# Moving VectorE's sums, one score group and the first tile's units in a pooled-attention plus feed-forward kernel

## Chip, cores, metric

The kernel runs on one core of one Trainium2 chip. The metric is the device time of one execution in microseconds (us). Executions of one kernel differ (the six of the kernel before in the comparison lie between 292.65 and 294.22 us), so medians of several are given. A profile shows one execution; its span is about 1.8 us shorter than the device time of the same execution (292.4 against 294.17).

## What is computed

Inputs q, k, v have the shape (8 batches, 8 heads, 576 positions, 64). Cut to what matters:

```python
k_p = k.reshape(B, H, 72, 8, D).mean(axis=3)       # pool 8 positions
v_p = v.reshape(B, H, 72, 8, D).mean(axis=3)
attn = softmax(scale * q @ k_p.T)                  # 576 x 72 per head
x = (attn @ v_p) as 4608 tokens x 512
h = x @ w_in                                       # 512 -> 2048
out = (h * cos(h)) @ w_out                         # 2048 -> 512
```

## The kernel before

The tokens go through in nine tiles of 512 (t=0 to 8). A tile has an **up stage** (128x512 matmuls by w_in, cosine on ScalarE, multiply on VectorE, which gives g) and a **down stage** (g by w_out). From t=1 on the down stage uses seven half-size products in place of eight, which need sums of quarters of g (g1 to g4) and of w_out; VectorE makes the sums of g, each in two halves (0 and 1). Between the products of tile t TensorE does the attention of batch t+1 in units u0 to u3 (scores, exponential on ScalarE, values, a multiply on VectorE that writes xT and frees a bank of PSUM, the memory that TensorE writes to) and a rest unit of batch t. GpSimd meanwhile pools k and v of batch t+2.

```python
def put_g12(i):                                     # two sums of 128x1024 bf16 each call
    f0, f1 = 4 * i, 4 * i + 4
    vec = nc.vector.tensor_tensor
    vec(out=g1[:, f0:f1], in0=g_part(0, 1, f0, f1), in1=g_part(1, 1, f0, f1), op=ADD)
    vec(out=g2[:, f0:f1], in0=g1[:, f0:f1], in1=g_part(0, 0, f0, f1), op=SUB)
# put_g3(i): g3 = g_part(0,0) - g_part(0,1);  put_g4(i): g4 = g_part(1,0) - g2
# ... in the up stage, after step n of 8 ...
if t == 1 and n == 6:
    put_g12(0)
if t > 1 and 3 <= n < 6:
    (put_g12, put_g3, put_g4)[n - 3](0)
# ... the down stage of t >= 1 (cut) ...
u0, u1, u2, u3 = [(b, us[i], banks[j]) for i, j in enumerate((2, 1, 0, 1))]
ur = (t, REST, banks[2])
product(0)
scores_of(u0, u1, u2)            # u2 needs bank 0, which the last multiply of g frees
product(1)
put_g12(1)
reads[0]()                       # copy of the first product out of PSUM (p_sb)
for i in range(0 if t == 1 else 1, 2):
    put_g3(i)
reads[1]()
for i in range(0 if t == 1 else 1, 2):
    put_g4(i)
values(*u0, later)
product(2); reads[2](); muls()   # muls: the multiply of the unit before
values(*u1, later)
product(3); reads[3](); muls()
values(*u2, later)
product(4); reads[4](); muls()
scores_of(ur, u3)                # u3 needs bank 1, which the multiply of u1 frees
# ... product(5) with the values of ur and u3 inside, product(6) ...
# ... the down stage of t == 0: (matmul number, unit) in order ...
fill = [(1, REST scores), (2, S0), (8, pool v), (8, REST values), (11, S1), (13, V0), (18, S2), ...]
```

The softmax here doesn't subtract the row's maximum and nothing guards it: scores larger than these inputs give would overflow.

## Time and profile before

| | before |
|---|---|
| device time, median (first 3 runs; with the 3 of the comparison) | 293.3 us; 293.49 us |
| TensorE busy in the profile | 280.6 of 292.4 us |
| VectorE, ScalarE, GpSimd busy | 79%, 71%, 51% |
| first tile's down stage | 20.24 us |
| down stage of t=1 | 18.42 us |
| a steady tile, start to start | 29.93 us |

A timeline line has start and duration in us, engine, line of the kernel, output and inputs, shape, count, and in brackets the idle time of the engine before it with what ended that. I take a tile's start as that of its first up matmul in TensorE's timeline; all stage lengths are differences of such starts.

The wait of 0.89 us at t=1 has its cause on VectorE. This is VectorE's timeline of the kernel before, at the end of the up stage of t=1:

```profile
66.74 1.23 DVE L331 TENSOR_TENSOR g_sb<-bank,cos 128x1024 bf16<-128x1024 f32 x1 [0.50 <-ACT cos L327]
67.88 0.68 DVE L359 TENSOR_TENSOR g<-g_sb 128x1024 bf16<-128x1024 bf16 x1
68.59 0.69 DVE L360 TENSOR_TENSOR g<-g,g_sb 128x1024 bf16<-128x1024 bf16 x1
69.20 1.22 DVE L331 TENSOR_TENSOR g_sb<-bank,cos 128x1024 bf16<-128x1024 f32 x1
```

Two sums (L359, L360) run before the last multiply, which frees the bank of the third score group.

### The profile page before, as it was taken

How to read it: one execution, taken by the hardware profiler on the slowest of the kernel's cores; microseconds unless marked ns; L12 is line 12 of the kernel's file. 1: busy time of each engine (PE TensorE's matmuls, PEld its weight loads, DVE VectorE, ACT ScalarE, POOL GpSimd, SP SyncE). 2: the span in 40 equal slices, each digit the busy share in tenths (PEclk: the TensorE clock that was granted, in tenths of full speed). 3: DMA queues.
4: the chain of work that ended last, by engine and by line, in shares of the span. 5: the costliest groups of instructions: out<-in, count | busy, mean ns of one | idle time of the engine just before them, and what ended most of it. 6: DMA issues, size and time to landing. Idle time of an engine off the chain costs nothing. (4 is left out here: it accounts for less than half of the span.)

```text
span 292.4 us, 5446 instructions
## 1 busy us (share of the span) xinstructions
PE 280.6 (96%) x2168; PEld 178.1 (61%) x2168; DVE 232.4 (79%) x314; ACT 208.1 (71%) x265; POOL 149.9 (51%) x145
## 2 busy tenths in 40 slices
PE   6989999998899999999999999999999999999994
PEld 2545544446764587458745884488547854884583
DVE  6458638879987988799879986988798879955972
ACT  3886888368877799679976987699769876536600
POOL 8553089993996359836983699329920000000000
PEclk9999999999999999999999999999999999999998
DMA  7999999557819692969196916694680050006014
GB/s 156 198 207 206 206 205 210 116 92 110 136 35 201 60 167 42 204 88 166 26 194 94 177 27 137 116 164 77 138 112 0 4 126 18 2 2 144 0 38 108
DMA packets 44489, 32.97 MB, mean 113 GB/s; under 512 B 22192, under 2 KB 40112, under 8 KB 44464
## 3 DMA queue, kind: packets, MB, share of 16 engines
q0 software_dynamic: 19744, 18.07, 39.4%
q1 hardware_dynamic: 24080, 14.03, 23.5%
q10 hardware_dynamic: 640, 0.52, 0.7%
q8 instruction: 17, 0.28, 0.4%
q14 instruction: 8, 0.07, 0.1%
HBM read 36.70 MB, written 9.44 MB: 158 GB/s over the span
## 5 line engine op out<-in xcount | busy, mean ns | idle before, releaser
L317 PE MATMUL bank<-xT,w_in_sb 128*128 128x512 bf16 x512 | 113.8, 379 | 0.0
L327 ACT ACTIVATE cos<-bank,half_pi 128x1024 f32<-128x1024 f32 x64 | 70.3, 1113 | 46.9 <-PE bank L317 46.3
L317 PEld LDWEIGHTS <-w_in_sb 128*128 128x128 bf16 x576 | 56.1, 98 | 65.8 <-issue 0.4
L331 DVE TENSOR_TENSOR g_sb<-bank,cos 128x1024 bf16<-128x1024 f32 x64 | 77.3, 1220 | 22.5 <-ACT cos L327 22.4
L151 POOL TENSOR_TENSOR half_sums<-kv_st 72x512 f32<-72x512 bf16 x48 | 57.6, 1228 | 26.1 <-DMA kv_st<-in_k_dram 25.7
L262 DVE TENSOR_TENSOR xT<-bank,inv 64x512 bf16<-64x512 f32 (+1 forms) x72 | 45.3, 629 | 12.9 <-ACT inv L258 11.8
L398 PEld LDWEIGHTS <-g 128*128 128x128 bf16 x512 | 49.0, 98 | 6.9 <-issue 1.2
L257 ACT ACTIVATE inv<-bank 64x512 f32<-64x512 f32 (+1 forms) x72 | 39.1, 544 | 11.9 <-PE bank L251 11.0
L398 PE MATMUL obank<-w,g 128*128 128x256 bf16 x368 | 43.6, 273 | 0.0
L398 PEld LDWEIGHTS <-g_sb 128*128 128x128 bf16 x384 | 36.8, 98 | 7.3 <-issue 1.2
L229 ACT ACTIVATE ex<-bank 72x1024 bf16<-72x1024 f32 (+1 forms) x40 | 35.2, 929 | 3.5 <-PE bank L222 3.3
L153 POOL TENSOR_TENSOR half_sums<-half_sums 72x512 f32<-72x512 f32 x24 | 29.9, 1267 | 0.0
L398 PE MATMUL obank<-w_out_sb,g_sb 128*128 128x256 bf16 x240 | 28.7, 273 | 0.0
L258 ACT ACTIVATE inv<-inv 128x512 f32<-128x512 f32 (+1 forms) x36 | 21.0, 583 | 1.1
L251 PE MATMUL bank<-ex,vz 72*128 72x256 bf16 (+1 forms) x176 | 20.1, 243 | 0.0
L222 PE MATMUL bank<-qT,kk 64*72 64x256 bf16 (+1 forms) x192 | 13.7, 252 | 3.4 <-DVE xT L262 1.7
L334 PE MATMUL obank<-w_out_sb,g_sb 128*128 128x512 bf16 x64 | 15.7, 380 | 0.7 <-DMA w_out_sb<-in_moe_w_out_dram 0.7
L251 PEld LDWEIGHTS <-vz 72*128 72x128 bf16 x176 | 13.7, 97 | 3.2 <-DVE xT L262 0.5
L156 POOL TENSOR_TENSOR kp<-half_sums 72x512 bf16<-72x512 f32 x12 | 15.4, 1304 | 0.5
L398 PE MATMUL obank<-w_out_sb,g 128*128 128x256 bf16 x112 | 15.6, 273 | 0.0
L398 PE MATMUL obank<-w,g_sb 128*128 128x256 bf16 x128 | 15.3, 273 | 0.0
L317 PE MATMUL obank<-xT,w_in_sb 128*128 128x512 bf16 x64 | 15.1, 379 | 0.0
(86 smaller groups left out, 254.9 us busy)
## 6 DMA issues: line engine op xcount, KB each, us to landing
out_dram<-o_two SPq DMA_DIRECT2D x64, 128.0 KB, 2.4
kv_st<-in_v_dram POOLq DMA_DIRECT2D x8, 576.0 KB, 13.0
kv_st<-in_k_dram POOLq DMA_DIRECT2D x7, 576.0 KB, 7.6
q_b<-in_q_dram POOLq DMA_DIRECT2D x6, 576.0 KB, 10.0
w_in_sb<-in_moe_w_in_dram POOLq DMA_DIRECT2D x4, 512.0 KB, 14.0
w_out_sb<-in_moe_w_out_dram POOLq DMA_DIRECT2D x4, 512.0 KB, 18.4
q_b<-in_q_dram POOLq DMA_DIRECT2D x4, 288.0 KB, 12.4
g_sb<-in_k_dram SPq DMA_DIRECT2D x1, 576.0 KB, 3.4
```

The lines of the kernel that those rows point to most:

```text
L151: add(out=s[:, h:h + 2], in0=x[:, h:h + 2, 0:4, :], in1=x[:, h:h + 2, 4:8, :], op=ADD)
L153: add(out=s[:, h:h + 4, 0:2, :], in0=s[:, h:h + 4, 0:2, :], in1=s[:, h:h + 4, 2:4, :], op=ADD)
L229: nc.scalar.activation(out=ex[:, 0:nh * n].rearrange("p (a n) -> p a n", a=2), in_=pair[:Sp, :, 0:nh * n // 2], func=ACTF.Exp, scale=scale ...
L251: nc.tensor.matmul(pair[:, hp, (i // 2) * n:(i // 2 + 1) * n], lhsT=vz[b % 2][:, pj, 2 * hp:2 * hp + 2, :].rearrange("p a d -> p (a d)"), ...
L257: nc.scalar.activation(out=inv[half[1 - hp]], in_=pair[half[1 - hp], hp, 0:w], func=ACTF.Ln)
L258: nc.scalar.activation(out=inv, in_=inv, func=ACTF.Exp, scale=-1.0)
L262: nc.vector.tensor_mul(out=x_out(b, u, half[hp]), in0=cols(pair[half[hp], hp, :], u), in1=cols(inv[half[1 - hp]], u))
L317: nc.tensor.matmul(h[j] if h is obanks else h[:, j, :], lhsT=w_in_sb[fc // 4][:, ki, (fc % 4) * 128:(fc % 4 + 1) * 128], rhs=xT[:, ki, t * ...
L327: nc.scalar.activation(out=c, in_=ps, func=ACTF.Sin, bias=half_pi[:, :1])
L331: nc.vector.tensor_mul(out=o, in0=ps, in1=c)
L334: nc.tensor.matmul(o, lhsT=g_sb[:, fc, ms * 128:(ms + 1) * 128], rhs=w_out_sb[fc // 4][:, fc % 4, :], start=(fc == 0), stop=(fc == FFCH - 1))
L398: mms.append(lambda bank=bank, first=first, g=g, w=w, fc=fc, p=p: nc.tensor.matmul(bank[p], lhsT=g(fc, p), rhs=w(fc), start=(first and fc ...
```

## The change

Its intent is to take the waits of TensorE away. It has four parts, called A to D here. **A**: `product(1, 0, 2)` before the scores, so these come two matmuls later. **B**: other places for the sums of half 0 at t=1. **C**: g4 of half 1 behind the multiplies of u1, in every tile. **D**: in the first tile, REST scores and S0 in one group, and S1 and V0 ahead of the ninth w_out matmul.

```diff
--- before.py
+++ after.py
@@ -353,19 +353,16 @@
     def g_part(f, t, f0, f1):
         return g_sb[:, f * HF + f0:f * HF + f1, t * HT:(t + 1) * HT]
 
-    def put_g12(i):
+    def put_g(k, i):
         f0, f1 = 4 * i, 4 * i + 4
-        vec = nc.vector.tensor_tensor
-        vec(out=g1[:, f0:f1], in0=g_part(0, 1, f0, f1), in1=g_part(1, 1, f0, f1), op=ADD)
-        vec(out=g2[:, f0:f1], in0=g1[:, f0:f1], in1=g_part(0, 0, f0, f1), op=SUB)
-
-    def put_g3(i):
-        f0, f1 = 4 * i, 4 * i + 4
-        nc.vector.tensor_tensor(out=g3[:, f0:f1], in0=g_part(0, 0, f0, f1), in1=g_part(0, 1, f0, f1), op=SUB)
-
-    def put_g4(i):
-        f0, f1 = 4 * i, 4 * i + 4
-        nc.vector.tensor_tensor(out=g4[:, f0:f1], in0=g_part(1, 0, f0, f1), in1=g2[:, f0:f1], op=SUB)
+        t1f1, t1f2, t2f1, t2f2 = [g_part(f, t, f0, f1) for t in range(2) for f in range(2)]
+        out, x, y, op = {1: (g1, t2f1, t2f2, ADD), 2: (g2, g1[:, f0:f1], t1f1, SUB), 3: (g3, t1f1, t2f1, SUB),
+                         4: (g4, t1f2, g2[:, f0:f1], SUB)}[k]
+        nc.vector.tensor_tensor(out=out[:, f0:f1], in0=x, in1=y, op=op)
+
+    def put_gs(*kis):
+        for k, i in kis:
+            put_g(k, i)
 
     def down_products(t):
 
@@ -543,10 +540,8 @@
                     puts[0](vec)
                     between = ((puts[1], act),)
             up_g(t, fp, between)
-            if t == 1 and n == 6:
-                put_g12(0)
-            if t > 1 and 3 <= n < 6:
-                (put_g12, put_g3, put_g4)[n - 3](0)
+            if 0 < t and 3 <= n < 6:
+                put_gs(*[(k, 0) for k in (((3,), (1,), ()) if t == 1 else ((1, 2), (3,), (4,)))[n - 3]])
             if 0 < t and b < B:
                 if n == 0:
                     q_transpose(b)
@@ -571,9 +566,10 @@
             exp_tables()
             fill = [(1, lambda: scores(t, REST, banks[2])), (16, lambda: values(t, REST, banks[1]))]
         if t == 0:
-            fill[1:] = [(2, S_(0, 0)), (8, lambda: pool_v_mm(1, banks[1])), (8, lambda: values(t, REST, banks[2])),
-                        (11, S_(1, 0)), (13, V_(0, 1)), (18, S_(2, 2)), (21, V_(1, 0, later)), (26, S_(3, 1)),
-                        (32, lambda: later.pop()()), (32, V_(2, 2)), (40, V_(3, 0))]
+            fill = [(2, fill[0][1]), (2, S_(0, 0)), (8, lambda: pool_v_mm(1, banks[1])),
+                    (8, lambda: values(t, REST, banks[2])), (8, S_(1, 0)), (8, V_(0, 1)),
+                    (18, S_(2, 2)), (21, V_(1, 0, later)), (26, S_(3, 1)), (32, lambda: later.pop()()),
+                    (32, V_(2, 2)), (40, V_(3, 0))]
         if t < FIRST:
             fi = 0
             for n, (ms, fc) in enumerate(mms):
@@ -615,18 +611,20 @@
             if rest:
                 exp_tables()
             product(0)
+            product(1, 0, 2)
             if steady:
                 scores_of(u0, u1, u2)
             elif rest:
                 scores_of(ur)
-            product(1)
-            put_g12(1)
+            product(1, 2)
+            if t == 1:
+                put_g(2, 0)
+            put_gs((1, 1), (2, 1))
             reads[0]()
-            for i in range(0 if t == 1 else 1, 2):
-                put_g3(i)
+            put_g(3, 1)
             reads[1]()
-            for i in range(0 if t == 1 else 1, 2):
-                put_g4(i)
+            if t == 1:
+                put_g(4, 0)
             if steady:
                 values(*u0, later)
             product(2)
@@ -637,6 +635,7 @@
             product(3)
             reads[3]()
             muls()
+            put_g(4, 1)
             if steady:
                 values(*u2, later)
             product(4)
```

I also built A, B, C and D as four edits of the kernel before. Their edits, shown with the experiments e1 (A), e2 (B), e3 (C) and e4 (D), together give the changed kernel's order of instructions, so the four parts are the whole change.

## The prediction

> **What bounds the kernel now.** I read the engine table first, then the list of TensorE's waits, then TensorE's timeline tile by tile. The table has each engine's busy time and share of the span.
>
> ```profile
> span 292.4 us, 5446 instructions
> PE 280.6 (96%) x2168; PEld 178.1 (61%) x2168; DVE 232.4 (79%) x314; ACT 208.1 (71%) x265; POOL 149.9 (51%) x145
> ```
>
> TensorE is the bound, and it is not busy for 292.4 - 280.6 = 11.8 us. The tail after its last matmul takes 292.4 - 288.4 = 4.0 us and the start 1.5 us; the change touches neither. The list of waits (total, times, longest) says what the rest is:
>
> ```profile
> PE bank L222 <- DVE xT L262: 1.7, 2, 1.4
> PE bank L222 <- DVE g_sb L331: 1.7, 6, 0.9
> PE obank L494 <- DVE g L438: 1.5, 1, 1.5
> PE obank L334 <- DMA w_out_sb<-in_moe_w_out_dram: 0.7, 1, 0.7
> ```
>
> The score matmuls (L222) of the next batch wait until VectorE has emptied the PSUM bank that they write. The timeline (start, duration, instructions, idle before) places these waits: first the second tile (t=1), then a steady one (t=2).
>
> ```profile
> 67.12 1.91 PE L398 MATMUL obank<-w_out_sb,g_sb 128*128 128x256 bf16 x16
> 68.96 0.63 PE L222 MATMUL bank<-qT,kk 64*72 64x256 bf16 x8
> 70.47 0.41 PE L222 MATMUL bank<-qT,kk 64*72 64x256 bf16 x4 [0.89 <-DVE g_sb L331]
> ...
> 81.01 0.41 PE L222 MATMUL bank<-qT,kk 64*72 64x256 bf16 x4 [1.40 <-DVE xT L262]
> ...
> 99.35 1.91 PE L398 MATMUL obank<-w_out_sb,g_sb 128*128 128x256 bf16 x16
> 101.19 0.63 PE L222 MATMUL bank<-qT,kk 64*72 64x256 bf16 x8
> 101.98 0.41 PE L222 MATMUL bank<-qT,kk 64*72 64x256 bf16 x4 [0.16 <-DVE g_sb L331]
> ```
>
> The 0.16 comes again in each of t=2 to 6, and at t=4 there is one more wait of 0.29 for an xT multiply. At t=7 and t=8 the trace shows no wait. So the change can reach at most 0.89 + 1.40 + 5 x 0.16 + 0.29 + 0.70 = **4.1 us**, 1.4% of 293.3.
>
> **What the Trainium skill says.** "Perfetto Trace Analysis", Optimization Strategy: look for the gaps on the bounding engine and for what releases them. That is the method here. "TensorEngine Tiling (Array Packing)", Key Properties: a change of tiling mode drains TensorE. The trace agrees: the 16 matmuls at 67.12 hand over to 64-row scores after 1.84 us, while the 16 at 70.81 hand over to 72-row ones after 1.76, so a switch costs about 0.09. "SBUF — State Buffer", Who interferes with whom: a VectorE instruction with two SBUF inputs contends with GpSimd instructions that read SBUF. The trace agrees: a sum over g of 128x1024 bf16 takes 0.68 us, but the two at 74.19 took 2.60 together, beside GpSimd's additions from 73.33.
>
> **The change part by part.**
>
> *A. First score group two matmuls later (t=1 to 6).* Two matmuls of 128x256 at 1.75/16 = 0.109 us, so 0.22 us, move ahead of the scores. In a steady tile the scores then start at 101.41 instead of 101.19, and the third group is due 0.63 later, at 102.04. Its bank is free at 100.70 + 1.22 = 101.92, and the group started 0.06 after that before. No wait is left. The number of mode switches stays. Gain 5 x 0.16 = **0.8 us** for t=2 to 6.
>
> *B. Other order on VectorE at t=1.* Before, the sums g1 and g2 of the first half ran at 67.88 to 69.28, ahead of the last multiply of g (69.20), whose cosine was ready at 68.44. They delayed it by 0.7. In the new order g3 and g1 of that half go into gaps in which VectorE waits for cosines (0.93 us idle before 63.28, 0.50 before 65.01), and g2 goes behind the multiply. That now runs from 68.49 to about 69.72. The third group is due at 68.96 + 0.22 + 0.63 = 69.8. Its wait of 0.89 goes.
>
> The second wait, 1.40, is for the multiply of the second unit, which ended at 79.57 + 1.39 = 80.96. I walk VectorE with starts 0.61 apart for independent sums and 0.73 for dependent ones: last multiply 68.49, g2 69.63, g1 70.24, g2 70.97, copy of the first product 71.58 to 72.27, g3, a read, g4 of the first half (0.7 alone, up to 1.3 beside GpSimd), a read to 75.4 at the latest, two multiplies to 76.8, a read to 77.5 (its product ends at 76.3), two multiplies to 78.95. TensorE wants that bank at about 78.8. So 1.40 shrinks to between 0 and 0.2. A **new wait** appears: the third product overwrites the bank that the copy reads until 72.27, and TensorE would be there at 72.11, so 0.2. Net at t=1: 0.89 + 1.40 - 0.2 - 0.15 = **1.95**, and with 0.1 of rounding either way I take 2.0 us.
>
> *C. g4 of the second half later (t=1 to 8).* One sum of 0.68 us leaves the place before the third read and goes behind the multiplies of the second unit. At t=4 this ends the 0.29 wait: two sums there took 1.67 and 1.04 instead of 0.68. Gain **0.3**. The price: at t=2 the sum now starts at about 110.6, beside GpSimd's additions (110.09 to 112.6), and its first reader, the ninth matmul of the sixth product (the built program waits there, not at the first), comes at about 112.1. With 0.68 it ends at 111.3; contended, with 1.3 to 1.8, at 111.9 to 112.4. I charge 0.05 to 0.1 for each of four tiles, **-0.3**. At t=6 and t=8 GpSimd is idle.
>
> *D. First tile.* The merged scores save one mode switch, 0.1, but then the pooling matmuls meet a bank that VectorE frees at 34.41 + 1.23 = 35.64 (they started at 35.69 before), so nothing comes of it. The two units moved forward fill the 0.70 wait for w_out group 2:
>
> ```profile
> 37.91 0.81 PE L334 MATMUL obank<-w_out_sb,g_sb 128*128 128x512 bf16 x3 [0.70 <-DMA w_out_sb<-in_moe_w_out_dram]
> 38.65 0.41 PE L222 MATMUL bank<-qT,kk 64*72 64x256 bf16 x4
> ```
>
> The scores run at 37.25 to 37.6, the values wait for pooled v (36.97 + 0.69 = 37.66) and end at 38.15, and w_out matmuls go on from there. Eight of them (8 x 0.216 = 1.73) reach group 1 at 39.9, where the kernel before was at 40.5. But group 1 has hardly landed: the transfers are back to back on a saturated queue (206 GB/s around there); one group is 0.524 MB, so 2.5 us, and I estimate from the landing of group 2 at 37.9 that groups 1 and 3 land at 40.45 and 43.0. Before, TensorE reached group 3 at 43.13 without a recorded wait. So the wait moves from group 2 to groups 1 and 3, and the gain is **0.1** of a possible 0.6.
>
> Sum: 0.8 + 2.0 + 0.3 - 0.3 + 0.1 = 2.9 us, so 293.3 - 2.9 = **290.4 us**.
>
> **The rivals.**
>
> 1. *All gaps close:* both transfers are early enough (0.4 more), no contention (0.3 more), t=1 perfect (0.3 more): 289.4. For it: each wait has one releaser, and VectorE is only 79% busy. Against: D's queue runs at its rate whatever TensorE does.
>
> 2. *VectorE gives it back:* g4 blocks behind GpSimd in every steady tile, the sixth product waits 0.3, and the later multiplies push the unit of the next tile (xT was ready at 117.14, its reader came at about 117.2, so slack is 0.06). That would lose 0.5 in each of four tiles: 292.4. For it: two weight sums at 54.1 and 55.9 beside GpSimd took 1.78 and 1.64. Against: after g4 ScalarE's chain sets the last multiplies anyway (idle 0.92 and 0.30 before them), which leaves VectorE 1.2 us of play.
>
> 3. *TensorE is not truly idle in the gaps:* its ends are modelled, so a wait of 0.16 may be partly an artefact. For it: "busy" is modelled. Against: the starts of the groups are recorded, and tiles with and without the extra 0.29 differ by it (29.93 against 30.33 us over two neighbouring tile starts, with t=4 also slower in its loads). This would make it 291.
>
> **Range and chances.** The runs before spread from 292.65 to 294.22, so a median of few may be 0.5 off. With rivals 1 and 2 at the ends plus some noise: 289.2 to 291.9. Faster by over 2% needs 5.9 us, more than all reachable waits together (4.1): 2%. Slower by over 2% would need a stall of a kind that the trace doesn't show: 1%.
>
> **What would show each step.** A: no wait of scores on g_sb at t=2 to 6, and tiles of about 13.81 + 15.96 = 29.77 us instead of 29.93. B: t=1's second half (67.12 to 85.54 before) takes 16.2 to 16.6 instead of 18.42 us, with a new wait of about 0.2 on the p_sb copy. C: the g4 instruction takes over 0.68 us at t=2 to 5 and TensorE waits for it little or not at all. D: the wait for w_out still totals 0.4 to 0.7, now at groups 1 and 3, and TensorE reaches t=1 at 53.2 rather than at 53.30. If w_out's wait vanishes, D is wrong upwards; if the sixth product waits for g4, or the first product of a tile for xT, C is wrong downwards.

## The result

The changed kernel takes **291.08 us** in the median (290.17 to 291.33, 6 runs), the kernel before 293.49 (292.65 to 294.22, 6 runs). The ratio is 0.9914, 95% interval 0.9893 to 0.9935. A ratio here is the mean time of one kernel's runs over that of the other's of the same rounds, so not quite the ratio of the medians. Executions over 1.5% slower than the fastest of the same kernel are left out of the means.

The engine table of the changed kernel, and its list of TensorE's waits (total, times, longest), with the start left out:

```profile
span 289.3 us, 5446 instructions
PE 281.1 (97%) x2168; PEld 178.5 (62%) x2168; DVE 233.1 (81%) x314; ACT 208.0 (72%) x265; POOL 149.9 (52%) x145
...
PE obank L395 <- DVE g_sb L331: 0.3, 1, 0.3
...
PE obank L334 <- DMA w_out_sb<-in_moe_w_out_dram: 0.2, 1, 0.2
```

The waits of score groups on g_sb and xT are gone. A new one on g_sb has come, and the one for w_out is smaller. TensorE's timeline of the changed kernel, t=1 first and t=2 after it:

```profile
67.36 2.13 PE L395 MATMUL obank<-w_out_sb,g_sb 128*128 128x256 bf16 x18
69.42 0.98 PE L222 MATMUL bank<-qT,kk 64*72 64x256 bf16 x12
...
71.87 0.60 PE L251 MATMUL bank<-ex,vz 72*128 72x256 bf16 x4
72.52 1.91 PE L395 MATMUL obank<-w,g 128*128 128x256 bf16 x16
...
78.72 0.55 PE L222 MATMUL bank<-qT,kk 64*72 64x64 bf16 x12
...
97.38 1.47 PE L395 MATMUL obank<-w_out_sb,g_sb 128*128 128x256 bf16 x12
99.13 0.83 PE L395 MATMUL obank<-w_out_sb,g_sb 128*128 128x256 bf16 x6 [0.27 <-DVE g_sb L331]
```

All twelve score matmuls of u0 to u2 now run in one piece (69.42), as do those of ur and u3 (78.72). Before the third product there is a gap that is too short for the list: the values at 71.87 take 4 x 0.109 = 0.44 us, so it could start at 72.31 and starts at 72.52. At t=2 the first product itself now waits 0.27.

Lengths of stages in us from TensorE's timelines, for the two kernels and for all experiments (t1 start is counted from the span's start):

| run | t0 down | t1 start | t1 down | t2 up | t2 down | t3 whole | t4 whole | span |
|---|---|---|---|---|---|---|---|---|
| before | 20.24 | 53.30 | 18.42 | 13.81 | 16.12 | 29.93 | 30.33 | 292.4 |
| changed, first | 19.96 | 53.55 | 16.11 | 13.91 | 16.21 | 29.72 | 29.71 | 289.3 |
| changed, after_again | 19.62 | 53.05 | 16.10 | 14.33 | 16.26 | 30.09 | 29.71 | 289.6 |
| changed, after_third | 19.61 | 52.77 | 16.10 | 14.24 | 16.21 | 29.99 | 29.71 | 289.1 |
| e1 (A alone) | 19.38 | 52.91 | 18.06 | 13.82 | 15.90 | 29.71 | 29.71 | 290.1 |
| e2 (B alone) | 19.38 | 53.45 | 16.25 | 13.94 | 16.36 | 29.94 | 29.93 | 290.3 |
| e3 (C alone) | 19.37 | 53.63 | 17.03 | 14.19 | 16.12 | 29.93 | 29.93 | 291.3 |
| e4 (D alone) | 20.13 | 52.93 | 18.48 | 13.82 | 16.12 | 29.93 | 29.93 | 291.7 |
| no_vz_add_t1 | 20.13 | 53.64 | 16.11 | 13.81 | 15.98 | 30.08 | 29.72 | 289.6 |
| after_no_w_out_wait | 19.61 | 52.81 | 16.10 | 14.07 | 16.39 | 30.08 | 29.72 | 289.2 |
| v1_both | 19.61 | 52.90 | 16.08 | 14.38 | 15.90 | 30.03 | 29.72 | 289.1 |
| f1 (changed without C) | 20.15 | 53.61 | 16.25 | 13.81 | 15.90 | 29.71 | 29.71 | 289.1 |
| f2 (C only from t=4) | 19.61 | 53.11 | 16.25 | 13.81 | 16.14 | 29.72 | 29.71 | 288.8 |
| f3 (f2 without D) | 19.62 | 52.81 | 16.25 | 14.12 | 16.25 | 29.71 | 29.71 | 288.9 |

In the first two profiles the span fell by 3.1 us. By stages: the start to the first w_out matmul lost 0.53 (33.06 to 33.59, code that the change does not touch), t0's down stage gained 0.28, t1's 2.31; t=2 lost 0.10 in its up and 0.09 in its down stage; t=3, 5 and 6 gained 0.21 to 0.22 each and t=4 0.62. The median time fell by only 2.41, because the profiled execution of before (294.17) was slower than the median of its kind.

### The profile page after: what moved, and what is told of

Read it like the earlier page. It is cut to its first block, busy times and chain, and to the rows that moved or that the text cites. A ratio compares the mean times of both kernels' runs of the same rounds, so it can differ in the third digit from the quotient of the medians.

```text
span 289.3 us, 5446 instructions
## 1 busy us (share of the span) xinstructions
PE 281.1 (97%) x2168; PEld 178.5 (62%) x2168; DVE 233.1 (81%) x314; ACT 208.0 (72%) x265; POOL 149.9 (52%) x145
## 4 chain that ended last, share of the span: by engine, by line
PE 70%; DVE 3%; ACT 0%; issue 0%
PE obank L395 31%; PE bank L317 27%; PE bank L251 4%; PE obank L317 4%; PE bank L222 3%; DVE g_sb L331 2%; PE bank L395 2%; DVE g L361 1%; ACT cos L327 0%; DVE o_two L411 0%
## 5 line engine op out<-in xcount | busy, mean ns | idle before, releaser
L151 POOL TENSOR_TENSOR half_sums<-kv_st 72x512 f32<-72x512 bf16 x48 | 54.5, 1162 | 26.2 <-DMA kv_st<-in_k_dram 25.8
L153 POOL TENSOR_TENSOR half_sums<-half_sums 72x512 f32<-72x512 f32 x24 | 31.8, 1345 | 0.0
L361 DVE TENSOR_TENSOR g<-g_sb 128x1024 bf16<-128x1024 bf16 x32 | 23.7, 740 | 0.5
L156 POOL TENSOR_TENSOR kp<-half_sums 72x512 bf16<-72x512 f32 x12 | 16.4, 1389 | 0.5
```

What stands on the lines that cost most here:

```text
L151: add(out=s[:, h:h + 2], in0=x[:, h:h + 2, 0:4, :], in1=x[:, h:h + 2, 4:8, :], op=ADD)
L153: add(out=s[:, h:h + 4, 0:2, :], in0=s[:, h:h + 4, 0:2, :], in1=s[:, h:h + 4, 2:4, :], op=ADD)
L361: nc.vector.tensor_tensor(out=out[:, f0:f1], in0=x, in1=y, op=op)
```

## The experiments

The theory at this point: A and B work as written, C's and D's gains are small, and the 0.27 at t=2 is a collision of VectorE with GpSimd. The rivals: the gain of t=1 is C's and not B's; C is a loss; D is worth its 0.6 us; the 0.27 is VectorE's own work.

### The four parts one at a time

All four ran on one chip against 11 runs of the kernel before (median 293.58, 292.77 to 294.64).

**A alone.**

```diff
             product(0)
+            product(1, 0, 2)
             if steady:
                 scores_of(u0, u1, u2)
             elif rest:
                 scores_of(ur)
-            product(1)
+            product(1, 2)
```

> Only the first score group moved two matmuls later. Theory: the 0.16 us wait of the third score group goes at t=2 to 6, so these tiles take 29.72 us from start to start instead of 29.93 (5 x 0.2 = 1.0 us), while t=1 gains nothing: its two waits end when VectorE is done (0.89 becomes about 0.67 because TensorE arrives 0.22 later, and the 1.40 stays as long as VectorE's chain sets it). Sum about 1.0 us of 293.5. Rival: the shift only moves idle time, because VectorE is late by a fixed amount after it: then t=2 to 6 stay at 29.93.

Measured: 292.52 us (292.03 to 293.34), ratio 0.9963 (0.9941 to 0.9985), so 0.0037 x 293.6 = 1.1 us. The waits of e1 at t=1, in TensorE's timeline:

```profile
70.08 0.41 PE L222 MATMUL bank<-qT,kk 64*72 64x256 bf16 x4 [0.67 <-DVE g_sb L331]
80.26 0.41 PE L222 MATMUL bank<-qT,kk 64*72 64x256 bf16 x4 [1.32 <-DVE xT L262]
```

The first wait shrank by exactly the two matmuls, 0.22, as expected. At t=2 to 6 no score group waits and the down stages take 15.90 instead of 16.12 us. So A is worth 5 x 0.22 = 1.1 us; the 0.16 that the waits showed was not the whole gap. I had expected nothing at t=1 and its stage got 0.36 shorter. VectorE's timeline of e1 shows where:

```profile
73.80 2.23 DVE L368 TENSOR_TENSOR g<-g_sb,g 128x1024 bf16<-128x1024 bf16 x2
```

In the kernel before this pair of sums took 2.60 us (74.19), so all that follows, the multiply that ends the second wait too, came 0.37 earlier. GpSimd's additions, which wait for their load, began at 73.83 in e1 and at 73.33 before, so the collision was a shorter one. Whether A brings that or the load's time is chance is not shown.

**B alone.** The third change, in the down stage, puts g2 of half 0 between `product(1)` and the sums of half 1, at t=1 only.

```diff
-            if t == 1 and n == 6:
-                put_g12(0)
+            if t == 1 and n == 3:
+                put_g3(0)
+            if t == 1 and n == 4:
+                g1 of half 0
 ...
-            for i in range(0 if t == 1 else 1, 2):
-                put_g3(i)
+            put_g3(1)
```

> Only the new places of g1, g2, g3 of the first half at t=1; g4 of both halves stays together before the third read. Theory: the wait of 0.89 shrinks to 0.1 to 0.2 (the last multiply ends 0.7 earlier), the wait of 1.40 shrinks to 0.3 to 0.7 because only the sums and not the last g4 have left the chain. t=1's second half takes 16.8 to 17.4 instead of 18.42 us, tiles 2 to 6 stay at 29.93. Sum about 1.2 us. Rival: the whole gain of t=1 comes from g4 of the second half; then this run gains 0.9 at most.

Measured: 292.16 us (290.98 to 292.68), ratio 0.9942 (0.9918 to 0.9965), 1.7 us. The waits of e2 in TensorE's timeline of t=1 and t=2:

```profile
69.89 0.41 PE L222 MATMUL bank<-qT,kk 64*72 64x256 bf16 x4 [0.16 <-DVE g_sb L331]
99.20 0.61 PE L398 MATMUL obank<-w_out_sb,g_sb 128*128 128x256 bf16 x4 [0.28 <-DVE g_sb L331]
```

t=1 gained 2.17 in its down stage, more than I expected: the wait of 1.40 is wholly gone without C. The rival that t=1 is C's gain falls. And the 0.28 at t=2 appears here, without C and without A: it comes with B.

**C alone.**

```diff
-            for i in range(0 if t == 1 else 1, 2):
-                put_g4(i)
+            if t == 1:
+                put_g4(0)
 ...
             reads[3]()
             muls()
+            put_g4(1)
```

> Only g4 of the second half moved behind the multiplies of the second unit, at t=1 to 8. Theory: at t=1 the 0.89 stays, the 1.40 shrinks by the sum's 0.7 to 1.3 us, to 0.1 to 0.7; at t=4 the wait of 0.29 (if this execution has it) is gone; TensorE never waits for the late g4 although it takes over 0.68 us beside GpSimd's additions at t=2 to 5. Sum 0.7 to 1.3 us. Rival (as predicted): each collision with GpSimd costs TensorE 0.05 to 0.1, so t=2 to 5 get longer than 29.93.

Measured: 292.78 us (292.24 to 293.08), ratio 0.9967 (0.9946 to 0.9987), 1.0 us. C alone takes the 1.40 away too (t=1's down stage 17.03). It gives 0.38 back in the up stage of t=2. Here are TensorE, then VectorE, GpSimd and ScalarE of e3 around that place:

```profile
80.79 1.22 PE L398 MATMUL obank<-w_out_sb,g 128*128 128x256 bf16 x8
...
86.57 3.61 PE L317 MATMUL bank<-xT,w_in_sb 128*128 128x512 bf16 x16 [0.21 <-DVE xT L262]
```

```profile
79.62 1.72 DVE L368 TENSOR_TENSOR g<-g_sb,g 128x1024 bf16<-128x1024 bf16 x1
...
85.13 1.39 DVE L262 TENSOR_TENSOR xT<-bank,inv 64x512 bf16<-64x512 f32 x2
```

```profile
79.53 2.94 POOL L153 TENSOR_TENSOR half_sums<-half_sums 72x512 f32<-72x512 f32 x2
```

```profile
83.91 0.63 ACT L258 ACTIVATE inv<-inv 128x512 f32<-128x512 f32 x1
```

The late g4 starts 0.09 us after a pair of GpSimd's additions and takes 1.72 instead of 0.68. All that VectorE does after it is late: the multiplies of u3 had their input at 83.91 + 0.63 = 84.54 and start at 85.13. The first up matmuls of t=2 that read this part of xT wait for them. The sixth product, where I had put the cost, came late too: the eight matmuls that hold its ninth one took 1.22 us instead of the usual 1.04, a wait of 0.18 at t=1 that the list does not show. So TensorE did wait for the late g4, against this run's expectation.

**D alone.**

```diff
-            fill[1:] = [(2, S_(0, 0)), (8, pool v), (8, REST values), (11, S_(1, 0)), (13, V_(0, 1)), ...
+            fill = [(2, fill[0][1]), (2, S_(0, 0)), (8, pool v), (8, REST values), (8, S_(1, 0)), (8, V_(0, 1)), ...
```

> Only the merged and moved units in the first tile. Theory: the w_out transfers set the pace, so the first tile's down stage (20.24 us from the first w_out matmul to t=1's start) gets 0.1 to 0.3 shorter and the wait for w_out moves from the ninth matmul to the seventeenth or the twenty-fifth. Everything from t=1 on stays as before, so its profile also shows how much t=4's 0.29 and the start vary by themselves. Sum 0.1 to 0.3 us, not told apart from noise by the times. Rival: the wait for w_out is filled for good, 0.6 us.

Measured: 294.08 us (293.64 to 294.79, 5 runs), ratio 1.0023 (0.9997 to 1.0049): no gain, if anything a loss. The w_out wait of e4 in TensorE's timeline:

```profile
40.15 0.59 PE L334 MATMUL obank<-w_out_sb,g_sb 128*128 128x512 bf16 x2 [0.36 <-DMA w_out_sb<-in_moe_w_out_dram]
```

The wait moved from the ninth to the seventeenth matmul, as the theory has it. But e1, e2 and e3, with the old order, had no recorded wait for w_out at all and a down stage of 19.38; whether TensorE meets the transfer differs from one execution to the next. In e1, e2 and e4 the tile t=4 took 29.71, 29.93 and 29.93, although nothing that touches its 0.29 wait was changed there in e2 and e4: that wait was chance of one execution.

The four gains sum to 1.1 + 1.7 + 1.0 - 0.7 = 3.1 us; the whole change measured 2.1 to 2.5. B and C both take the same 1.40 away, and it can only be had once.

### The new wait at t=2

**Changed kernel without GpSimd's additions of v for batch 3.** The result is wrong. The skipped call issues seven additions, not six as the expectation says.

```diff
-            pool_add(b + 1, "v")
+            if t != 1:
+                pool_add(b + 1, "v")
```

> The changed kernel without GpSimd's pooling additions of v for batch 3 (six instructions, issued at t=1 and running at t=1 and 2). Wrong result on purpose: batch 3 uses stale pooled v. Theory: the first sum over g at t=2 takes 0.69 instead of 1.29 us, and TensorE's wait of 0.27 for g_sb at t=2 is gone: it was a collision of VectorE with GpSimd. Rival: VectorE is late at t=2 for its own work, then the wait stays.

In the changed kernel (first profile) VectorE and GpSimd at t=2 were:

```profile
92.45 1.29 DVE L361 TENSOR_TENSOR g<-g_sb 128x1024 bf16<-128x1024 bf16 x1
93.78 0.69 DVE L361 TENSOR_TENSOR g<-g,g_sb 128x1024 bf16<-128x1024 bf16 x1
```

```profile
91.93 1.27 POOL L159 TENSOR_TENSOR vz<-half_sums 72x512 bf16<-72x512 f32 x1
```

Without the additions the same two sums on VectorE:

```profile
92.54 0.69 DVE L361 TENSOR_TENSOR g<-g_sb 128x1024 bf16<-128x1024 bf16 x1
93.27 0.69 DVE L361 TENSOR_TENSOR g<-g,g_sb 128x1024 bf16<-128x1024 bf16 x1
```

The wait of 0.27 is gone, t=2's up stage takes 13.81 and its down stage 15.98. So it was the collision: with B, TensorE and VectorE reach t=2 two us earlier, but GpSimd waits for its own load (its last addition ended at 91.04 + 1.26 = 92.30 before and at 91.93 + 1.27 = 93.20 after), and the first sum of t=2 (at 94.52 before, at 92.45 after) now falls beside it. In this up stage one multiply and one sum per step fill VectorE (1.13 + 0.60 us between starts, of a step's 1.73), so 0.6 us of delay stays until the seventh step, whose g the first product needs. One run (291.4 us), one profile, state unknown.

**Two more moves.** g4 of half 0 behind the second read in every tile; the copy of the first product ahead of g2 of half 1.

```diff
-  ... ((3,), (1,), ()) if t == 1 else ((1, 2), (3,), (4,))
+  ... ((3,), (1,), ()) if t == 1 else ((1, 2), (3,), ())
-            put_gs((1, 1), (2, 1))
+            put_g(1, 1)
             reads[0]()
+            put_g(2, 1)
 ...
-            if t == 1:
-                put_g(4, 0)
+            put_g(4, 0)
```

> The changed kernel with two more moves: g4 of the first half goes behind the second read in every tile (as the change does at t=1 only), and the copy of the first product goes before g2 of the second half. Theory: VectorE has 1.14 us idle behind the second read at t=2, and the sum that leaves the up stage lets it catch up even when GpSimd delays a sum there: the wait of 0.27 of TensorE for g_sb at t=2 goes, and the 0.2 before the third product at t=1 goes. t=2's halves take 13.81 and 15.90 instead of 13.91 and 16.21, t=1's second half 15.9 instead of 16.11. Sum 0.5 to 0.6 us against the changed kernel. Rival: the sum collides with GpSimd in its new place and a new wait appears for the third read; then no gain.

Measured: 290.85 us (290.71 to 291.01, 5 runs), ratio to before 0.9897 (0.9869 to 0.9925). t=2's down stage fell to 15.90 and has no wait, as expected, but its up stage took 14.38 and not 13.81: 0.37 of that came in its first up matmuls, which wait for xT behind the late g4 of half 1, as in e3. The move of the copy brought next to nothing (t=1's down stage 16.08 instead of 16.10). At t=3 the late g4 took 1.83 us and the ninth matmul of the sixth product came 0.29 late, the cost that the prediction had charged (eight matmuls of 0.109 would take 0.87 and the tail of one, 1.04 as elsewhere). TensorE, then VectorE of this kernel:

```profile
139.31 1.33 PE L395 MATMUL obank<-w_out_sb,g 128*128 128x256 bf16 x8
```

```profile
138.14 1.83 DVE L361 TENSOR_TENSOR g<-g_sb,g 128x1024 bf16<-128x1024 bf16 x1
```

**The changed kernel again.**

> The changed kernel unchanged, on the chip of v1_both, for comparison of the two and to see whether the 0.27 at t=2 and the 0.18 for w_out come again. Theory: both come again within 0.2, since both follow from the order of instructions and from the transfers' pace. Rival: they are chance of one execution.

Measured: 291.42 us (290.71 to 292.81), ratio 0.9920 (0.9890 to 0.9950). The waits from t=2 on, in TensorE's timeline:

```profile
85.02 3.61 PE L317 MATMUL bank<-xT,w_in_sb 128*128 128x512 bf16 x16 [0.17 <-DVE xT L262]
99.03 0.83 PE L395 MATMUL obank<-w_out_sb,g_sb 128*128 128x256 bf16 x6 [0.27 <-DVE g_sb L331]
115.65 3.61 PE L317 MATMUL bank<-xT,w_in_sb 128*128 128x512 bf16 x16 [0.21 <-DVE xT L262]
```

The 0.27 comes again. The w_out wait does not. And C's cost, which the first profile of the changed kernel did not have, shows at both tile boundaries here. At t=2 the up stage is 14.33 - 13.81 = 0.52 longer; 0.33 of it comes before the 25th up matmul, where xT is waited for, and the rest in the last 32, behind the sum that meets GpSimd (e2, without C, has 0.13 there). At t=3 it is 30.09 - 29.72 = 0.37. Its cause on VectorE and GpSimd at t=1 is the one of e3:

```profile
78.29 1.50 DVE L361 TENSOR_TENSOR g<-g_sb,g 128x1024 bf16<-128x1024 bf16 x1
...
83.58 1.39 DVE L262 TENSOR_TENSOR xT<-bank,inv 64x512 bf16<-64x512 f32 x2
```

**The changed kernel without two transfers.** w_out groups 1 and 3 are the tiles of groups 0 and 2; the result is wrong.

```diff
-    ... name=f"w_out_sb{i}") for i in range(4)]
+    ... name=f"w_out_sb{i}") for i in (0, 2)]
+    w_out_sb = [w_out_sb[0], w_out_sb[0], w_out_sb[1], w_out_sb[1]]
-    for cg in (2, 1, 3):
-        load_w_out(cg)
+    load_w_out(2)
```

> The changed kernel with w_out groups 1 and 3 taken from the tiles of groups 0 and 2, so that these two transfers do not exist. Wrong result on purpose. Theory: the transfers set the pace of the first tile's down stage, so without them it takes 0.2 to 0.5 us less than with them, about 19.6 us, and no wait for w_out is left. Rival: the down stage is as long as with them (19.96 in the first profile), so that something else sets it.

Measured: 290.62 us (290.48 to 291.01, 4 runs), t0's down stage 19.61. That is the same as in the executions of the changed kernel that met no transfer (19.62, 19.61), and 0.23 more than the old order without a wait (19.38). So the 19.61 is D's own: moved forward, S1 must wait for ScalarE and V0 for VectorE. The merged scores do save time (1.01 us from the first to the third w_out matmul, against 1.23 in e1), but the pooling matmuls then start 1.62 instead of 1.40 us after that third one, for their bank is not free yet, as the prediction had it. The median time of this run is 0.8 us below that of the changed kernel in the same call (291.42), more than the waits for w_out that any profile of the new order shows (up to 0.37); why is open. TensorE of the changed kernel, first profile:

```profile
37.33 0.41 PE L251 MATMUL bank<-ex,vz 72*128 72x64 bf16 x8
37.78 0.41 PE L222 MATMUL bank<-qT,kk 64*72 64x256 bf16 x4
38.24 0.61 PE L251 MATMUL bank<-ex,vz 72*128 72x256 bf16 x4
```

and what it waits for there, on ScalarE and on VectorE:

```profile
36.22 1.50 ACT L229 ACTIVATE ex<-bank 72x512 bf16<-72x512 f32 x2
```

```profile
37.50 0.69 DVE L178 CAST vz<-bank 72x512 bf16<-72x512 f32 x1 [0.74 <-PE bank L176]
```

The exponentials end at 37.72 and the scores start at 37.78; the pooled v is there at 38.19 and the values start at 38.24. In the old order these 0.2 us are filled with w_out matmuls. D pays a sure 0.23 against a wait that comes only in some executions, and the wait came with D too (0.18 to 0.37 at group 1 in four of its eight profiles).

### Undoing C, and D

All four ran on one chip, with 12 runs of the kernel before (median 293.71, 292.77 to 294.64).

**f1: the changed kernel, g4 of half 1 back before the third read in all tiles.**

```diff
             reads[1]()
             if t == 1:
                 put_g(4, 0)
+            put_g(4, 1)
 ...
             muls()
-            put_g(4, 1)
```

> The changed kernel with g4 of the second half back before the third read in every tile (at t=1 too); all else as changed. Theory: the late g4 collides with GpSimd (1.1 to 1.8 instead of 0.68 us) and pushes the xT multiplies of the last unit behind the first up matmuls of the next tile; so without it the up stages of t=2 and t=3 take 13.8 to 13.95 instead of the 14.33 and 14.19 of the second profile of the changed kernel, with no wait for xT. t=1's down stage stays at 16.1 to 16.3 (the new order alone had cut it to 16.25). Gain against the changed kernel of the same call 0.3 to 0.9 us. Rival: without the late g4 the wait of the last score group for xT (0.29 at t=4, or up to 1.4 at t=1) comes back and the time is as the changed one's or above.

Measured: 290.81 us (290.21 to 291.21), ratio 0.9898 (0.9875 to 0.9921). Both boundaries are clean (up stages 13.81), and t=4 has no wait. Undoing C costs 0.15 at t=1 (16.25 against 16.10).

**f2: the late g4 from t=4 on.** As f1, with `if t < 4` at the first and `if t >= 4` at the second place. The last unit of batch t+1 starts at token 576(t+1) + 256, and the next tile ends at token 512(t+2); so the next tile reads it only where 64(t+1) < 256, that is at t=1 and 2.

> The changed kernel with the late g4 only from t=4 on, where the last unit's tokens lie beyond the next tile's columns. Theory: as f1_undo_late_g4 for t=1 to 3, and no wait at t=4 to 6 in any execution: 0.3 to 0.9 us faster than the changed kernel. Rival: the late g4 costs nothing on average, then it is within 0.2 us of the changed kernel.

Measured: **290.19 us** (289.95 to 290.57), ratio 0.9881 (0.9860 to 0.9903). That is 0.6 below f1, which the edit does not explain: from t=3 on the two profiles have the same stage lengths. Its only recorded wait after the start is the collision at t=2, 0.19 us:

```profile
98.65 0.83 PE L395 MATMUL obank<-w_out_sb,g_sb 128*128 128x256 bf16 x6 [0.19 <-DVE g_sb L331]
```

**f3: f2 with D undone.**

> f2_late_g4_from_t4 with the first tile's units in the old places. Theory: the w_out transfers land at a time set by the start of the program, so t=1 starts at about 53.0 to 53.5 us from the span's start with either order and the times agree within 0.3 us; without a wait for w_out the down stage of the first tile takes 19.38 us in the old order and 19.61 in the new one. Rival: the moved units are worth 0.3 us or more in the median.

Measured: 290.56 us (290.28 to 291.35), ratio 0.9898 (0.9877 to 0.9919). That is 0.37 above f2 in the median, so the rival's mark of 0.3 us was reached. But the two profiles hardly differ (spans 288.9 and 288.8), and e4 against the kernel before went the other way (0.5 us slower with D). The down stage of the first tile took 19.62 and not the 19.38 expected without a wait; the transfer of group 1 was probably met again, in a wait too short for the list: the five matmuls that hold the seventeenth take 1.46 us, where e1 has 1.24. The start of t=1 is what D is to bring forward. With D (after, after_again, after_third, e4, no_vz_add_t1, v1, f1, f2) it came at 53.20 on average, without D (before, e1, e2, e3, f3) at 53.22, each spread over 0.8 to 0.9 us. The stage itself averages 19.85 with D and 19.60 without; the code ahead of it, which D does not touch, happened to end 0.28 earlier in D's profiles. So no profile shows a gain of D, and whether it gains, loses or does nothing is not settled by these runs.

**The changed kernel a third time.**

> The changed kernel unchanged on this chip, for comparison with the other three. Theory: up stages at t=2 or t=3 of 14.2 to 14.4 us with a wait for xT in most executions, 0.2 to 0.5 us at t=2's down stage for g_sb. Rival: the first profile (13.91 and 13.82) is the usual case.

Measured: 291.50 us (290.92 to 292.03), ratio 0.9927 (0.9906 to 0.9948). C's cost is there again: of the 14.24 - 13.81 = 0.43 at t=2, 0.25 comes before the 25th up matmul; of the 29.99 - 29.72 = 0.27 at t=3, 0.13 comes there and 0.14 in the sixth product (1.18 instead of 1.04 us). The 0.27 for g_sb at t=2 is there too. Every run of f2 (at most 290.57) is below every run of the changed kernel (at least 290.92) in this call. So f2 beats both kernels: 1.3 us below the changed one and 3.5 below the one before in the medians. The profiles show 0.3 to 0.8 of the 1.3 us (spans 288.8 against 289.1 and 289.6). The profiled execution of f2 was its slowest of six (290.57), though, and that of the changed kernel in this call its fastest (290.92), so they understate the difference.

## Why the prediction was right or wrong

The time (290.4 predicted, 291.08 measured) lay in the range, and the direction was right: 2.9 us were forecast, 2.41 measured. That the sum came so near is partly luck, for two errors offset each other: A and t=1 brought about 0.6 us more than forecast, and the late g4 and the unforeseen collision at t=2 together took some 0.9 us (average of the three profiles of the changed kernel) where C was booked as costing nothing net. By its own steps:

- **What bounds, and the ceiling of 4.1 us: right**, and it decided the chances. No version tried came near 2%; the best gained 1.2%.
- **A: right, a little too small.** 0.8 was forecast, 1.1 came. The step took the recorded 0.16 for the gap; the stage got 0.22 shorter. The recorded 0.29 at t=4 was likewise 0.40 in stage length, so the prediction's third rival misreads 29.93 against 30.33 as differing by it.
- **B: right.** 1.95 to 2.0 was forecast, 2.31 came at t=1 (16.11 us, just under the 16.2 to 16.6 given). Both waits went, and the new gap of 0.2 before the third product came where it was said (0.21). e2 shows that B does this without C (2.17); what it then lost at t=2 left 1.7 in its time.
- **C's gain of 0.3: wrong.** The 0.29 at t=4 was chance; e2 and e4 do not have it. A gain that one execution shows in one tile was booked as if it came each time.
- **C's cost: the place was right, a second place was missed.** I charged 0.3 to the ninth matmul of the sixth product in four tiles. Seven profiles have the late g4 at t=1 to 3 (the three of the changed kernel, e3, v1, no_vz_add_t1, after_no_w_out_wait). In six of them that matmul came late in one or two tiles, by 0.05 to 0.29 us; no list of waits shows it, only the length of the group of eight matmuls does. The step did not see that the late g4 also delays VectorE's multiplies for the next tile: in six of the seven the first up matmuls of t=2 or t=3 came up to 0.37 late for xT. Together this is 0 to 0.87 us a profile, 0.57 on average. The seven profiles without the late g4 there show neither delay. Rival 2 had named the second way, with a slack of 0.06, but for four tiles; only two boundaries can be hit. Its 292.4, by the way, lies outside the range that was to cover it.
- **D: forecast 0.1, no gain shown.** The wait moved to group 1 as said, but was 0.18 in the first profile and not 0.4 to 0.7. What was missed is that a wait for a transfer at that place depends on the execution, and that moved units bring waits of their own (0.23).
- **Not foreseen: the wait at t=2**, 0.27 recorded. The walk stopped at t=1's end. With TensorE and VectorE two us ahead and GpSimd not, other sums meet GpSimd's additions. This follows from B's success. In the three profiles of the changed kernel it made t=2 0.4 to 0.5 us longer; in f1, where the first sum came as the addition was ending (92.65 and 91.52 + 1.26 = 92.78), nothing.
- Rival 3, that the gaps are an artefact of modelled ends, falls: filling 0.22 took 0.22 off five stages.

Still open: the sign of D, and the 0.6 us between the medians of f1 and f2, which no stage that the edit touches explains.

## What to carry to other kernels

When a bounding engine is idle only in small gaps, sum the gaps first: that is the ceiling, whatever is moved. After removing a wait, walk on into the next stage with each engine's new time, for engines that did not move along (here GpSimd, gated by its loads) will meet others at new places. When work is put later on an engine, list what waits behind it there, and not only its own reader: here that second cost was the larger one. Look at several executions before booking a wait that shows in one place only, and prefer putting deferred work where its engine idles over putting it in front of a multiply that something already waits for.

## What the Trainium skill lacked or had wrong

- "SBUF — State Buffer", Who interferes with whom: it says that a VectorE instruction with two SBUF inputs contends with a GpSimd instruction that reads SBUF, and these runs agree. That the second one to issue blocks until the first is done, as the page's section "Summary: rules for kernel authors" has it, fits: in e3 GpSimd's first addition of about 1.25 us would end at 79.53 + 1.25 = 80.78, and the sum of 0.68 us ended at 79.62 + 1.72 = 81.34. What the page does not spell out is a sum that meets a row of additions, where both sides pay: GpSimd's pair grew too, to 2.94 us from the 2.49 that it took in f3. This may be the same rule applied twice. Sums took up to 1.83 us.
- "TensorEngine Tiling (Array Packing)", Key Properties: it says that a change of tiling mode drains TensorE, without a cost. Here it is about 0.09 us from 128-row matmuls to 64-row ones (16 matmuls hand over after 1.84 instead of 1.75 us).
- "Perfetto Trace Analysis", Optimization Strategy: it names too little SBUF or PSUM as a possible reason for a gap that repeats. Here the repeated 0.16 us per tile was a matter of instruction order alone; two matmuls moved ahead closed it (16.12 to 15.90 us per stage) with the same buffers.
